# Long convolution and mixture of experts on one core: folded forward transform, y copied whole and combined a step later, loads in a ring

## Chip, cores and metric

One core of a Trainium2 chip. The metric is the device time of one execution in microseconds (us), of one launch.

## The reference, cut to what matters

```python
# B, S, D = 4, 11456, 128     E, F = 8, 1024     N = B * S
h_filt = (np.maximum(pos_emb @ w1, 0.0) @ w2) * np.exp(-0.01 * pos)[:, None]
u = x * v
y = irfft(rfft(u, n=2 * S) * rfft(h_filt, n=2 * S))[:, :S]     # along the sequence, per channel
t = (x * y).reshape(N, D)                                      # what the experts get
logits = t @ w_gate + modality_bias[modality_id]
e_idx = np.argmax(logits, axis=1)
gate_w = softmax(logits)[np.arange(N), e_idx]
out[e_idx == e] = gate_w * (np.maximum(t @ w1[e], 0.0) @ w2[e])
```

All inputs are fp32; `x` and `v` are 4 sequences of 11456 positions and 128 channels.

## The kernel before

The transform of a sequence is split into 90 x 64 points (`N1`, `N2`) and done by matmuls against constant tables. Its state is one tile `A` in SBUF (`[128, 90, 2, 128]`). The program goes through stages: the filter and its spectrum; the forward transform of sequence 0 alone (table `FIRST`); a **middle** stage (spectral product, 64-point transforms both ways); an **outer** stage, in which the inverse transform and the routing of sequence b-1 run beside the forward transform of sequence b (table `OUTER`); middle and outer in turn until sequence 3 is alone (table `LAST`); then the experts.

An outer stage has 16 steps q (`NQ`) of 8 channels. For each q:

- `load_x` (L653) and `load` (L444) bring x, u and v of q to SBUF on SP's queue, each a tile `seq` [128, 1024] from a pool of 11 buffers of 4 KB per partition (`NA`) that y and others share.
- `product` (L449), on DVE: u times v, in place. The two ways of a sequence lie in the two halves of the partitions, its two blocks `blk` in the two halves of the columns.
- `forward` (L461): for both halves h of q, four channels, two blocks and two ways: fp32 matmuls `s` of 128 rows by 64 columns, 90 moving columns (64 PE records in a step). ACT copies them to `A` (L464), one copy for each half.
- `turn0`, `turn1` (L659): 16 PE transposes `wt` out of `A` for the inverse transform, 4 copies on ACT (L660).
- `inverse` (L668): `py`, two accumulators [128, 512] in PSUM. ACT copies the second to SBUF (L671), DVE adds and subtracts it with the first, which it reads from PSUM (L673, L674), and multiplies by x into `xo` (L675): 90 points come from two halves of 45.
- routing: `half` (L716) transposes the q's half of `xo` (`xT`, copied by ACT, L718); every second step `logits` (`pl`, L724; ACT copy `lT`, L727), `lturn` (`lt`, L733), `biased` (L739), `choice` (DVE from `mx` L747 to L768, with an exponential `ex` on ACT, L751), and `send` (matmuls `pr`, `pn`, L784 to L789, positions on DVE, L791 to L798).
- POOL scatters rows of `xo` to the experts' lists by indirect DMAs (L267), each released by a DVE instruction that `paced` names.

The order is written by hand. A table names each part with its offset:

```python
OUTER = ("turn0:1 turn1:1 lturn:3 biased:3 forward:2 load_x:0 product:1 half:2 choice:3 "
         "inverse:1 logits:2 send:4 load:0 store:4 places:5")
```

`steps` (L142) issues in step t, in the table's order, part f of q = t - offset. All of PE, ACT, DVE, POOL and SP keep that order, each in its own queue. `early` and `overlapped` with `EA`, `OV`, `F1` to `F3` let a stage begin some steps before the one ahead has ended.

Of the kernel before, what the change touches and what calls it, by code (L numbers as in the profile page):

```python
# [12 lines left out]
F32 = mybir.dt.float32  # L13
# [27 lines left out]
NQ = N2 // 4  # L41
# [28 lines left out]
NA, NXO = 11, 3  # L70
# [109 lines left out]
def hyena_moe_kernel(ctx: ExitStack, tc: tile.TileContext, a: dict, out: bass.AP,  # L180
# [177 lines left out]
    with ExitStack() as cv:  # L358
# [8 lines left out]
        def new_a(name, dt=F32):  # L367
            return st.tile([D, 1024], dt, tag="a", name=name, bufs=NA)


        rings = keepp.tile([D, 12 * GW], F32, name="rings")
        A = keepp.tile([D, N1, 2, D], F32, name="A")
# [65 lines left out]
        def forward_stages(b):  # L438
            kept = {}

            def load(q):
                for name in ("u", "v"):
                    t = kept[q, name] = new_a("seq")
                    sp.dma_start(t, a[name][b, q])  # L444

            def product(q):

                u = kept[q, "u"]
                s = dve.tensor_mul(u, u, kept.pop((q, "v")))  # L449
                paced(s, 2)  # L450

            def transform(q):

                u = kept.pop((q, "u")).rearrange("p (b d n) -> p b d n", b=2, n=N2)
# [14 lines left out]
        def filter_stages():  # L469
# [3 lines left out]
            def load(q):  # L473
                t = kept[q, "emb"] = new_a("emb")[:, 0:512]
                sp.dma_start(t, a["pos_emb"][q])

            def hidden(q):
# [5 lines left out]
                r = new_a("r")[:, 0:512].rearrange("p (m f) -> p m f", m=8)  # L483
# [84 lines left out]
        def middle_stages(b):  # L568
# [16 lines left out]
            def spectrum(g):  # L585
# [3 lines left out]
                for q in range(n):  # L589
                    for c in range(2):  # L590
# [10 lines left out]
                part = [new_a("part")[:, 0:n * 4 * D].rearrange("p (c q b d) -> p c q b d", c=2, b=2, d=D)  # L601
                        for _ in range(2)]
                more = new_a("more")[:, 0:n * 4 * D].rearrange("p (i c q d) -> p i c q d", i=2, c=2, d=D)
# [43 lines left out]
        def inverse_stages(b):  # L647
# [3 lines left out]
            def load(q):  # L651
                t = kept[q] = new_a("seq")
                sp.dma_start(t, a["x"][b, q])  # L653
# [8 lines left out]
            def transform(q):  # L662
# [15 lines left out]
            return load, turn, transform  # L678
# [24 lines left out]
        def route_stages(b):  # L703
# [17 lines left out]
            def logits(o):  # L721
# [4 lines left out]
                lT = kept[o] = new_a("lT")[:, 0:4 * PU]  # L726
# [90 lines left out]
        def outer_steps(b):  # L817
# [3 lines left out]
            if b > 0:  # L821
                load_x, turn, itransform = inverse_stages(b - 1)
                rturn, logits, lturn, biased, choice, send, store, places = route_stages(b - 1)
                todo = {
                    "load_x": load_x, **by_block("turn", turn), "inverse": itransform,
# [43 lines left out]
        def place(name, shape, dt=F32):  # L869

            n = math.prod(shape)
            if not scratch or scratch[-1][1] + n > 512:
                scratch.append([new_a("scratch")[:, 0:512], 0])
# [257 lines left out]
def device_inputs(inputs):  # L1131
    arrays = {name: np.ascontiguousarray(inputs[name]) for name in _INS}
    tile4 = lambda a: a.reshape(D, 2, NQ, 4, -1).transpose(2, 0, 1, 3, 4).reshape(NQ, D, -1)
    chan8 = lambda a: a.reshape(2, 64, 2, N2, NQ, 8).transpose(4, 2, 1, 0, 5, 3).reshape(NQ, D, -1)
    for name, of, order in (("x", "x", tile4), ("u", "x", chan8), ("v", "v", chan8)):
        arrays[name] = np.ascontiguousarray(
            np.stack([order(spread(np.asarray(a))) for a in inputs[of]]))
# [27 lines left out]
```

## Time and profile before

| | us |
|---|---|
| median of 3 runs | 2307.93 (2306.96 to 2316.54) |
| the profiled execution | 2316.88 |
| its span, first to last instruction | 2315.1 |

Busy share of the span: PE 95%, PE's weight loads 76%, DVE 73%, ACT 53%, POOL 44%. The mean granted TensorE clock is 0.981. These are means over stages with different limits; the table of stages tells more. Stages in us from the start of the span: filter 0 to 103, forward transform of sequence 0 to 149, middle to 265, outer to 400, middle to 527, outer to 667, middle to 795, outer to 938, middle to 1063, sequence 3 alone to 1211, experts to the end. A step of an outer stage is read from two neighbouring `s` in PE's timeline.

### The profile page before, as it was taken

To read this page: it belongs to the slowest core of one execution; us is meant where nothing else is said; L and a number is where in the kernel's file an instruction comes from. 1 tells how busy PE (TensorE), PEld (TensorE's weight loads), DVE (VectorE), ACT (ScalarE), POOL (GpSimd) and SP (SyncE) were. 2 spreads that over 40 slices of the span, in tenths; PEclk is the share of its full clock that TensorE was granted. 3 is DMA by queue.
4 is the path that set the end of the run, shared out by engine and by line. 5 is a ranking of instruction groups with operands and counts; after the bars stand their busy time and mean duration, and the time that the engine had idled before them with its cause. 6 is when DMAs were issued, how large, how long until landed. Compare 5 with 4: busy or idle time off the path is not lost. (4 is left out here: it accounts for less than half of the span.)

```text
span 2315.1 us, 49859 instructions
## 1 busy us (share of the span) xinstructions
PE 2193.5 (95%) x18746; PEld 1758.8 (76%) x18746; DVE 1688.5 (73%) x2862; ACT 1224.2 (53%) x2245; POOL 1015.4 (44%) x1012
## 2 busy tenths in 40 slices
PE   8989999899989999898879999999999999999998
PEld 8877776677657766675447788888888888888898
DVE  2359666995679666894657677777777877777797
ACT  4632465126532365223435666666666666666676
POOL 0116300595438754396533455555553333333333
PEclk9999999999999999998879999999999999999999
DMA  9666675777867787674546622222222111111111
GB/s 309 244 253 211 220 228 177 249 252 267 272 217 256 253 267 254 213 254 143 166 133 200 219 69 76 70 67 69 67 65 73 47 47 47 47 45 46 40 42 34
DMA packets 168635, 359.22 MB, mean 155 GB/s; under 512 B 32237, under 2 KB 65497, under 8 KB 168389
## 3 DMA queue, kind: packets, MB, share of 16 engines
q1 hardware_dynamic: 141445, 295.83, 40.0%
q0 software_dynamic: 26784, 60.12, 7.4%
q8 instruction: 150, 2.46, 0.4%
q14 instruction: 96, 0.79, 0.1%
q10 hardware_dynamic: 160, 0.03, 0.0%
HBM read 271.44 MB, written 84.83 MB: 154 GB/s over the span
## 5 line engine op out<-in xcount | busy, mean ns | idle before, releaser
L1048 DVE SCALAR_TENSOR_TENSOR hl<-ph,hh 128x512 fp32r<-128x512 f32 x724 | 497.0, 690 | 217.0 <-ACT hh L1047 149.0
L1084 POOL DMA_INDIRECT out<-ot,idx x362 | 360.4, 996 | 603.6 <-DVE ot L1081 518.0
L1047 ACT ACTIVATE hh<-ph 128x512 fp32r<-128x512 f32 x724 | 433.0, 601 | 336.4 <-PE ph L1044 254.9
L267 POOL DMA_INDIRECT xs<-back,to x360 | 386.9, 1075 | 273.1 <-DVE y L673 126.1
L1042 PE MATMUL ph<-xh,wh 128*128 128x512 f32 (+1 forms) x792 | 303.4, 383 | 2.1 <-ACT wh L1013 1.2
L1065 PE MATMUL po<-hh,wh 128*128 128x512 f32 (+1 forms) x792 | 295.1, 373 | 5.4 <-ACT hh L1047 4.5
L641 ACT COPY A<-pw 128x512 f32<-128x512 f32 (+1 forms) x184 | 97.2, 580 | 379.6 <-PE pw L637 375.9
L1067 PE MATMUL po<-hl,wh 128*128 128x512 f32 (+1 forms) x792 | 295.4, 373 | 1.4 <-DVE hl L1048 1.4
L1043 PE MATMUL ph<-xh,wl 128*128 128x512 f32 (+1 forms) x792 | 295.3, 373 | 0.3 <-DVE wl L1014 0.3
L1044 PE MATMUL ph<-xl,wh 128*128 128x512 f32 (+1 forms) x792 | 295.5, 373 | 0.1
L1066 PE MATMUL po<-hh,wl 128*128 128x512 f32 (+1 forms) x792 | 294.7, 372 | 0.0
L613 DVE TENSOR_TENSOR part<-pz,rings 128x1024 f32<-128x1024 f32 (+1 forms) x184 | 211.5, 1190 | 5.3 <-POOL part L618 5.3
L593 PE MATMUL pz<-A,rings 128*64 128x256 f32 x1440 | 180.3, 393 | 31.5 <-issue 13.8
L637 PE MATMUL pw<-rings,part 64*128 64x128 f32 x2880 | 203.5, 280 | 5.7 <-POOL part L618 5.6
L637 PEld LDWEIGHTS pw<-rings,part 64*128 64x128 f32 x2880 | 177.8, 189 | 40.3 <-issue 29.5
L608 POOL TENSOR_TENSOR more<-more 128x256 f32<-128x256 f32 (+1 forms) x84 | 68.3, 813 | 284.0 <-DVE more L605 274.9
L461 PE MATMUL s<-fwd,seq 128*64 128x90 f32 x4096 | 174.2, 243 | 12.4 <-issue 4.4
L461 PEld LDWEIGHTS s<-fwd,seq 128*64 128x64 f32 x4096 | 163.1, 137 | 23.5 <-issue 6.5
L659 PEld LDWEIGHTS wt<-ident,A 128*90 128x90 f32 x1024 | 125.2, 185 | 66.3 <-issue 37.9
L1065 PEld LDWEIGHTS po<-hh,wh 128*128 128x128 f32 x792 | 149.6, 189 | 33.1 <-ACT hh L1047 5.6
L1067 PEld LDWEIGHTS po<-hl,wh 128*128 128x128 f32 x792 | 149.5, 189 | 30.0 <-DVE hl L1048 3.8
L1044 PEld LDWEIGHTS ph<-xl,wh 128*128 128x128 f32 x792 | 149.8, 189 | 26.7 <-DVE xl L1029 0.5
(172 smaller groups left out, 3788.5 us busy)
## 6 DMA issues: line engine op xcount, KB each, us to landing
rings<-hs SPq DMA_DIRECT2D x88, 512.0 KB
seq<-in_u SPq DMA_DIRECT2D x64, 512.0 KB
seq<-in_v SPq DMA_DIRECT2D x64, 512.0 KB
seq<-in_x SPq DMA_DIRECT2D x64, 512.0 KB
back<-xr SPq DMA_DIRECT2D x72, 325.0 KB
xr<-xo SPq DMA_DIRECT2D x62, 365.6 KB
rings<-in_c_b SPq DMA_DIRECT2D x88, 256.0 KB
rings<-in_c_c SPq DMA_DIRECT2D x88, 256.0 KB
```

The lines of the kernel that those rows point to most:

```text
L267: s = pool.indirect_dma_start(out=xs, out_offset=bass.IndirectOffsetOnAxis(ap=ix, axis=0), in_=src, in_offset=None, bounds_check=E * R - 1 ...
L461: pe.matmul(v[64 * c:64 * c + 64, blk, j], u[:, blk, 4 * h + j], fwd[:, c], start=True, stop=True)
L637: pe.matmul(pw[par][:, to:to + D], t[at], k["c"][at, q, c], start=i == 0, stop=i == len(terms) - 1)
L1042: pe.matmul(p, k[0, "h"][:, f:f + D], k["xh"], start=True, stop=False)
L1043: pe.matmul(p, k[0, "l"][:, f:f + D], k["xh"], start=False, stop=False)
L1044: pe.matmul(p, k[0, "h"][:, f:f + D], k["xl"], start=False, stop=True)
L1047: act.activation(hh, ph, AF.Relu)
L1048: dve.scalar_tensor_tensor(hl, ph, 0.0, hh.bitcast(F32), op0=ALU.max, op1=ALU.subtract)
L1065: pe.matmul(po, k[1, "h"][:, f], hh[:, t], start=g == 0, stop=False)
L1066: pe.matmul(po, k[1, "l"][:, f], hh[:, t], start=False, stop=False)
L1067: pe.matmul(po, k[1, "h"][:, f], hl[:, t], start=False, stop=g == NCH - 1)
L1084: s = pool.indirect_dma_start(out=out, out_offset=bass.IndirectOffsetOnAxis(ap=k["idx"][:, j:j + 1], axis=0), in_=ot[:, j, :], in_offset=N ...
```

## The change

1. **Forward on quarters, from sequence 1 on.** The product goes to a tile `p`; then `of` = [p0+p1 | p0-p1] over the two column halves: the add on DVE, the subtraction on POOL (sequence 1, and even q later) or on DVE (odd q of sequences 2 and 3). Each matmul of `forward` has 45 rows, beginning at partition 0 or 64, by 64 columns: a quarter of the array, in the order (0,0), (1,1), (1,0), (0,1) of `parts`. The number of matmuls stays. Sequence 0 keeps the old form (`whole`). For sequences 1 to 3 the host lays out u and v with the blocks in the partition halves and the ways in the column halves.
2. **y in one copy, combined a step later.** ACT copies both accumulators of `py` in one instruction of 128x1024. The new part `combine` has offset 2 in `OUTER` (first in rank) and 3 in `LAST`; it adds, forms the difference as -2 y1 + sum, and multiplies by x. `half` keeps its offset, so it now stands in the same step as the `combine` whose `xo` it reads.
3. **Loads in a ring.** x, u and v go round 7 slots of a tile `around` (sequence 0: 9 slots for u and v), two more hold `of`; the middle stages use the same slots. The first load of sequence 0 is issued from step 13 instead of 0 (`FIRST`), and outer stages begin 2 instead of 3 steps early (`EA`).

```diff
-OUTER = ("turn0:1 turn1:1 lturn:3 biased:3 forward:2 load_x:0 product:1 half:2 choice:3 "
+OUTER = ("combine:2 turn0:1 turn1:1 lturn:3 biased:3 forward:2 load_x:0 product:1 half:2 choice:3 "
          "inverse:1 logits:2 send:4 load:0 store:4 places:5")
-LAST = ("inverse:2 turn0:1 half:3 lturn:4 biased:4 logits:3 turn1:1 choice:4 load_x:1 send:5 store:5 places:6")
+LAST = ("combine:3 inverse:2 turn0:1 half:3 lturn:4 biased:4 logits:3 turn1:1 choice:4 load_x:1 send:5 "
+        "store:5 places:6")
-FIRST = "forward:17 load:0 product:16"
+FIRST = "forward:17 product:16 load:13"
-GD, OV, EA, EM = 2, 2, 3, 4
+GD, OV, EA, EM = 2, 2, 2, 4
-NA, NXO = 11, 3
+NA, NU, NS, NXO = 9, 7, 2, 3
...
         def new_a(name, dt=F32):
-            return st.tile([D, 1024], dt, tag="a", name=name, bufs=NA)
+            return st.tile([D, 1024], dt, tag="a", name=name, bufs=NS)
...
+        def rows_of(src, n=NU):
+            at = counts["rows", n] = (counts.get(("rows", n), -1) + 1) % n
+            t = around[:, at]
+            sp.dma_start(t, src)
+            return t
...
             def load(q):
                 for name in ("u", "v"):
-                    t = kept[q, name] = new_a("seq")
-                    sp.dma_start(t, a[name][b, q])
+                    kept[q, name] = rows_of(a[name][b, q], NU if b else NA)
             def product(q):
-                u = kept[q, "u"]
-                s = dve.tensor_mul(u, u, kept.pop((q, "v")))
-                paced(s, 2)
+                if b == 0:
+                    of = kept[q, "of"] = kept.pop((q, "u"))
+                    paced(dve.tensor_mul(of, of, kept.pop((q, "v"))), 2)
+                    return
+                u, v = kept.pop((q, "u"))[0:PU], kept.pop((q, "v"))[0:PU]
+                p, of = new_a("p")[0:PU], around[:, NU + q % (NA - NU)]
+                paced(dve.tensor_mul(p, u, v), 2)
+                dve.tensor_add(of[0:PU, 0:512], p[:, 0:512], p[:, 512:1024])
+                eng = pool if b == 1 or q % 2 == 0 else dve
+                eng.tensor_sub(of[0:PU, 512:1024], p[:, 0:512], p[:, 512:1024])
+                kept[q, "of"] = of
             def transform(q):
...
+                whole = [(c, blk, slice(0, D), blk) for blk in range(2) for c in range(2)]
+                parts = [(c, blk, slice(64 * blk, 64 * blk + HALF), c)
+                         for c, blk in ((0, 0), (1, 1), (1, 0), (0, 1))]
...
-                        for blk in range(2):
-                            for c in range(2):
-                                pe.matmul(v[64 * c:64 * c + 64, blk, j], u[:, blk, 4 * h + j],
-                                          fwd[:, c], start=True, stop=True)
+                        for c, blk, at, of_c in parts if b else whole:
+                            pe.matmul(v[64 * c:64 * c + 64, blk, j], of[at, of_c, 4 * h + j],
+                                      fwd[at, c], start=True, stop=True)
...
-                y = new_a("y")
-                act.copy(y[:, 512:1024], py[:, 1])
+                y = kept[q, "y"] = new_a("y")
+                act.copy(y, py.rearrange("p c m -> p (c m)"))
+            def combine(q):
+                y = kept.pop((q, "y"))
                 n = 2 if b == nb - 1 else 1
-                paced(dve.tensor_add(y[:, 0:512], py[:, 0], y[:, 512:1024]), 2 * n - 1)
-                dve.tensor_sub(y[:, 512:1024], py[:, 0], y[:, 512:1024])
-                paced(dve.tensor_mul(xo_of(b, q // 2)[:, :, q % 2, :, 0:D], four(y),
-                                     four(kept.pop(q))), n)
+                paced(dve.tensor_add(y[:, 0:512], y[:, 0:512], y[:, 512:1024]), 2 * n - 1)
+                dve.scalar_tensor_tensor(y[:, 512:1024], y[:, 512:1024], -2.0, y[:, 0:512],
+                                         op0=ALU.mult, op1=ALU.add)
+                paced(dve.tensor_mul(xo_of(b, q // 2)[0:PU, :, q % 2, :, 0:D], four(y[0:PU]),
+                                     four(kept.pop(q)[0:PU])), n)
...
```

What this does to the order of two steps in the third outer stage. On **DVE before**, from the last combination of a step with a choice through the step with the positions (`ro`, L791, and on) of a group:

```order
L673 TENSOR_TENSOR y<-py,y 128x512
L674 TENSOR_TENSOR y<-py,y 128x512
L675 TENSOR_TENSOR xo_84<-y,seq 128x2x4x128
L449 TENSOR_TENSOR seq<-seq 128x1024
L673 TENSOR_TENSOR y<-py,y 128x512
L674 TENSOR_TENSOR y<-py,y 128x512
L675 TENSOR_TENSOR xo_85<-y,seq 128x2x4x128
L791 TENSOR_TENSOR ro<-pr,base 109x128
```

On **DVE now**, the same step (`p` is the product, `around<-p` the folded sum; L821 to L828 are the positions):

```order
L702 TENSOR_TENSOR y<-y 128x512
L703 SCALAR_TENSOR_TENSOR y<-y 128x512
L705 TENSOR_TENSOR xo_84<-y,around 109x2x4x128
L467 TENSOR_TENSOR p<-around 109x1024
L468 TENSOR_TENSOR around<-p 109x512
L821 TENSOR_TENSOR ro<-pr,base 109x128
L822 TENSOR_TENSOR base<-base,pn 128x8
L823 TENSOR_TENSOR ro<-ro,oh_94 109x128
L825 TENSOR_REDUCE sl<-ro 109x16
L828 TENSOR_TENSOR ix_87<-sl,small 109x4x4
L702 TENSOR_TENSOR y<-y 128x512
```

Before, the step began with the product, and its own combination (the second) and the positions followed; now it begins with the combination of the `py` of the step ahead, and the positions stand ahead of the next combination.

On **PE now**, the end of that step (L746 is `half`, which reads the `xo` that L705 writes; the others as named above):

```order
L484 MATMUL s_9514<-fwd,around 64x90 x16
L746 MATMUL xT<-ident,xo_83 128x109 x8
L693 MATMUL py<-rings,inv 64x512 x4
L754 MATMUL pl<-rings,wg 32x436 x4
L814 LDWEIGHTS both
L814 MATMUL pr<-oh_94,both 128x128
```

PE's order is that of before; but its `xT` now reads what DVE writes in the same step.

## Rows read from the trace of the kernel before

**Rows 1.** The span cut at the stages of the program: us from the start, length, busy time and number of instructions of each engine, granted TensorE clock (1.00 is full speed), DMA share and GB/s. From above: the forward transform of sequence 0, the first and the second outer stage, and the inverse transform and routing of sequence 3 alone.

```profile
103.00:149.00 46.00, 41.07 (x1024) 40.22 (x1024) 18.61 (x18) 23.83 (x32) 0.66 (x2) 1.00 0.86 329
...
265.00:400.00 135.00, 132.41 (x1631) 95.26 (x1632) 87.56 (x177) 86.45 (x158) 0.00 (x0) 1.00 0.66 213
...
527.00:667.00 140.00, 133.78 (x1630) 95.35 (x1629) 86.73 (x177) 84.44 (x155) 67.34 (x62) 1.00 0.77 255
...
1063.00:1211.00 148.00, 119.71 (x608) 67.40 (x608) 73.61 (x174) 64.17 (x124) 72.44 (x70) 0.84 0.49 139
```

**Rows 2.** The timeline of PE through two steps of the first outer stage: start, us, engine and line, operation, out<-in, tile and shapes, count. A step starts with `s`.

```profile
321.97 2.70 PE L461 MATMUL s<-fwd,seq 128*64 128x90 f32 x64
324.60 0.97 PE L716 MATMUL xT<-ident,xo 109*128 109x109 f32 x8
325.50 1.94 PE L668 MATMUL py<-rings,inv 90*64 90x512 f32 x8
327.37 2.01 PE L659 MATMUL wt<-ident,A 128*90 128x128 f32 x16
329.31 2.70 PE L461 MATMUL s<-fwd,seq 128*64 128x90 f32 x64
...
334.70 0.94 PE L724 MATMUL pl<-rings,wg 128*32 128x436 f32 x8
335.57 0.23 PE L784 MATMUL pr<-oh,both 109*128 109x128 bf16 x1
...
335.73 2.75 PE L659 MATMUL wt<-ident,A 128*90 128x128 f32 x16
338.57 0.69 PE L733 MATMUL lt<-ident,lT 128*109 128x128 f32 x4
339.19 1.00 PE L461 MATMUL s<-fwd,seq 128*64 128x90 f32 x20
```

**Rows 3.** The same view at the start of the second outer stage, before its routing has begun: the `s` rows of two neighbouring steps.

```profile
532.98 2.70 PE L461 MATMUL s<-fwd,seq 128*64 128x90 f32 x64
...
540.31 2.70 PE L461 MATMUL s<-fwd,seq 128*64 128x90 f32 x64
```

**Rows 4.** The same view in the third outer stage: one `wt` and the same place two steps later, and between them the `xT` of the step with a `pr`, and the `pn` at the end of that group.

```profile
840.58 2.00 PE L659 MATMUL wt<-ident,A 128*90 128x128 f32 x16
...
845.52 0.97 PE L716 MATMUL xT<-ident,xo 109*128 109x109 f32 x8
...
849.28 0.18 PE L789 MATMUL pn<-sc,both 109*128 109x8 bf16 x1
...
858.61 0.59 PE L659 MATMUL wt<-ident,A 128*90 128x128 f32 x3
```

**Rows 5.** The timeline of DVE over the two steps of Rows 2 (in brackets the idle time before an instruction, and what ended it): combination, product, the choice from `mx` to the gate's column, and the positions from `ro` on.

```profile
322.09 0.28 DVE L739 TENSOR_TENSOR lg<-lt,bs 109x128 f32<-109x128 f32 x1
322.29 1.22 DVE L449 TENSOR_TENSOR seq<-seq 128x1024 f32<-128x1024 f32 x1
323.43 0.36 DVE L747 TENSOR_REDUCE mx<-lg 109x16 f32<-109x128 f32 x1
...
326.57 0.37 DVE L763 TENSOR_REDUCE se<-ex 109x16 f32<-109x128 f32 x1 [0.72 <-ACT ex L751]
...
327.35 0.12 DVE L768 TENSOR_SCALAR xo<-small 109x16 f32<-109x16 f32 x1
328.11 0.69 DVE L673 TENSOR_TENSOR y<-py,y 128x512 f32<-128x512 f32 x1 [0.65 <-ACT y L671]
328.84 0.69 DVE L674 TENSOR_TENSOR y<-py,y 128x512 f32<-128x512 f32 x1
329.56 1.23 DVE L675 TENSOR_TENSOR xo<-y,seq 128x1024 f32<-128x1024 f32 x1
330.71 1.22 DVE L449 TENSOR_TENSOR seq<-seq 128x1024 f32<-128x1024 f32 x1
...
338.03 0.28 DVE L791 TENSOR_TENSOR ro<-pr,base 109x128 f32<-109x128 f32 x1
...
339.32 0.28 DVE L739 TENSOR_TENSOR lg<-lt,bs 109x128 f32<-109x128 f32 x1
```

**Rows 6.** Groups by line and shape in the middle stage of sequence 0: operation, out<-in, count, busy us and mean ns: operations from SBUF to SBUF on 128x512, on POOL and on DVE.

```profile
L618 POOL TENSOR_TENSOR part<-part 128x512 f32<-128x512 f32 x20 | 34.4, 1719 | 16.9 <-DVE part L613 16.1 <-DMA rings<-in_c_b 0.8
...
L617 DVE TENSOR_TENSOR part<-part 128x512 f32<-128x512 f32 x22 | 15.2, 692 | 0.8
```

**Rows 7.** The same view of ACT in the first outer stage.

```profile
L464 ACT COPY A<-s 128x720 f32<-128x720 f32 x32 | 24.3, 760 | 24.1 <-PE s L461 24.1
...
L671 ACT COPY y<-py 128x512 f32<-128x512 f32 x16 | 9.5, 594 | 17.4 <-PE py L668 15.9 <-issue 1.6
```

**Rows 8.** The timeline of ACT in the third outer stage: the second copy out of `s` in a step with a choice.

```profile
858.21 0.76 ACT L464 COPY A<-s 128x720 f32<-128x720 f32 x1 [2.73 <-PE xT L716]
```

**Rows 9.** The timeline of DVE there: the sum of exponentials, which waits for ACT's `ex`.

```profile
841.77 0.39 DVE L763 TENSOR_REDUCE se<-ex 109x16 f32<-109x128 f32 x1 [2.70 <-ACT ex L751]
```

**Rows 10.** The timeline of DVE in the forward transform of sequence 0: a product.

```profile
109.28 1.23 DVE L449 TENSOR_TENSOR seq<-seq 128x1024 f32<-128x1024 f32 x1 [1.15 <-DMA seq<-in_v]
```

**Rows 11.** The timeline of DVE in the stage with sequence 3 alone.

```profile
1125.15 0.69 DVE L673 TENSOR_TENSOR y<-py,y 128x512 f32<-128x512 f32 x1 [2.56 <-ACT y L671]
```

**Rows 12.** The page's list of DMA issues: out<-in, queue, operation, count, KB each.

```profile
seq<-in_u SPq DMA_DIRECT2D x64, 512.0 KB
```

More of the change, by code (lines that the diff above doesn't have):

```diff
@@ L473, in load @@
             def load(q):
-                t = kept[q, "emb"] = new_a("emb")[:, 0:512]
+                t = kept[q, "emb"] = next_a()[:, 0:512]
                 sp.dma_start(t, a["pos_emb"][q])
@@ L482, in hidden @@
                               start=True, stop=True)
-                r = new_a("r")[:, 0:512].rearrange("p (m f) -> p m f", m=8)
+                r = next_a()[:, 0:512].rearrange("p (m f) -> p m f", m=8)
                 dve.scalar_tensor_tensor(
@@ L598, in spectrum @@
                 h = k["h"]
-                part = [new_a("part")[:, 0:n * 4 * D].rearrange("p (c q b d) -> p c q b d", c=2, b=2, d=D)
-                        for _ in range(2)]
-                more = new_a("more")[:, 0:n * 4 * D].rearrange("p (i c q d) -> p i c q d", i=2, c=2, d=D)
+                at = 3 * ((g + 1) % 3)
+                part = [around[:, at + i, 0:n * 4 * D].rearrange("p (c q b d) -> p c q b d", c=2, b=2, d=D)
+                        for i in range(2)]
+                more = around[:, at + 2, 0:n * 4 * D].rearrange("p (i c q d) -> p i c q d", i=2, c=2, d=D)
                 for i in range(2):
@@ L651, in load @@
             def load(q):
-                t = kept[q] = new_a("seq")
-                sp.dma_start(t, a["x"][b, q])
+                if q == 0:
+                    counts.pop(("rows", NU), None)
+                kept[q] = rows_of(a["x"][b, q])
             def turn(q, blk):
@@ L669, in transform @@
                                   start=True, stop=True)
-                y = new_a("y")
-                act.copy(y[:, 512:1024], py[:, 1])
+                y = kept[q, "y"] = new_a("y")
+                act.copy(y, py.rearrange("p c m -> p (c m)"))
+            def combine(q):
+                y = kept.pop((q, "y"))
                 n = 2 if b == nb - 1 else 1
-                paced(dve.tensor_add(y[:, 0:512], py[:, 0], y[:, 512:1024]), 2 * n - 1)
-                dve.tensor_sub(y[:, 512:1024], py[:, 0], y[:, 512:1024])
-                paced(dve.tensor_mul(xo_of(b, q // 2)[:, :, q % 2, :, 0:D], four(y),
-                                     four(kept.pop(q))), n)
-            return load, turn, transform
+                paced(dve.tensor_add(y[:, 0:512], y[:, 0:512], y[:, 512:1024]), 2 * n - 1)
[3 more added lines that the diff above has]
+                                     four(kept.pop(q)[0:PU])), n)
+            return load, turn, transform, combine
         md = []
@@ L725, in logits @@
                               xT_t[:, g].rearrange("p h n -> p (h n)"), start=True, stop=True)
-                lT = kept[o] = new_a("lT")[:, 0:4 * PU]
+                lT = kept[o] = st.tile([D, 4 * PU], F32, tag="lT", name="lT", bufs=1)
                 act.copy(lT, pl[:, 0:4 * PU])
@@ L871, in place @@
             n = math.prod(shape)
-            if not scratch or scratch[-1][1] + n > 512:
-                scratch.append([new_a("scratch")[:, 0:512], 0])
+            if not scratch:
+                scratch.append([rings[:, 4096:6144], 0])
             of, lo = scratch[-1]
@@ L1133, in device_inputs @@
     tile4 = lambda a: a.reshape(D, 2, NQ, 4, -1).transpose(2, 0, 1, 3, 4).reshape(NQ, D, -1)
-    chan8 = lambda a: a.reshape(2, 64, 2, N2, NQ, 8).transpose(4, 2, 1, 0, 5, 3).reshape(NQ, D, -1)
+    swap = lambda a: np.stack([a[0], a[1, :, ::-1]])
+    chan8 = lambda a: swap(a.reshape(2, 64, 2, N2, NQ, 8)).transpose(4, 0, 1, 2, 5, 3).reshape(NQ, D, -1)
+    ways8 = lambda a: a.reshape(2, 64, 2, N2, NQ, 8).transpose(4, 2, 1, 0, 5, 3).reshape(NQ, D, -1)
     for name, of, order in (("x", "x", tile4), ("u", "x", chan8), ("v", "v", chan8)):
-        arrays[name] = np.ascontiguousarray(
-            np.stack([order(spread(np.asarray(a))) for a in inputs[of]]))
+        arrays[name] = np.ascontiguousarray(np.stack([
+            (ways8 if name != "x" and b == 0 else order)(spread(np.asarray(a)))
+            for b, a in enumerate(inputs[of])]))
     pos = spread(np.asarray(inputs["pos_emb"])).reshape(2, 64, 2, NQ, 4, -1)
```

10 lines of the change are left out of this document (7 added, 3 removed).

## Prediction

> **What bounds the kernel now.** The mean shares say PE, but stages differ, so I read the span cut by stage first [rows 1]. In an outer stage PE is busy 132.41 of 135.00 and 133.78 of 140.00 us at full clock, DVE 87.56 and 86.73: PE bounds. In the stage of sequence 3 alone PE is busy 119.71 of 148.00 at a clock of 0.84, and no engine is full: a chain bounds. Experts, filter and middle stages are not touched but for buffers.
>
> Second, PE's timeline of two steps [rows 2]: `s` to `xT` takes 324.60 - 321.97 = 2.63 us, `xT` 0.90, `py` 1.87, `wt` 1.94, so 7.34 a step; every second step adds `pl` 0.87, `pr` and `pn` 0.16, `lt` 0.62. That is 16.33 of work in the 17.22 that two steps take (321.97 to 339.19); the rest is a stall inside `wt`. Before the routing begins a step takes 540.31 - 532.98 = 7.33 [rows 3]: PE alone. In the third outer stage two steps take 858.61 - 840.58 = 18.03 [rows 4]; I use that for the second stage as well, which lasts 5 us longer than the first [rows 1], as 13 such steps longer by 0.4 would.
>
> Third, DVE's timeline [rows 5], because the change loads DVE. Combination: 0.73 + 0.72 + 1.15 to the next start, 2.60. Product 1.14. Choice, `mx` to the gate's column: 327.35 + 0.12 - 323.43 - 0.72 of waiting = 3.32. Positions 339.32 - 338.03 = 1.29. `lg` 0.20. DVE's `y` waits for ACT in the first of these steps (0.65), so today it follows PE; nothing on PE waits for DVE for long, because `xT` reads an `xo` of the step before.
>
> **The forward transform.** The 64 records of a step stay, with the same 90 moving columns; only the array's part differs. Today two column halves run side by side, in 2.63 us. With four quarters at once I halve that: 1.3 less, of which I take 1.24, a first start and the gaps being kept. Bounds: nothing saved, or 1.3. The nearest row for four at once is `pl`: four column tiles, 8 records of 436 columns, mean 541 ns by itself, all done in 0.94 us [rows 2]; so four parts do overlap, even in fp32, where a matmul is two records. I take the upper value since that row is the same thing in columns.
>
> The Trainium skill ("TensorE: Matmul & The Clock Gate", Part 3, What overlaps and what doesn't) says that matmuls start and end strictly in program order. Here the two passes of an fp32 matmul come one behind the other for one quarter, so by it the second would hold back the next quarter, and the saving would be near nothing; `pl`, issued in the same manner, speaks against such a loss.
>
> Fold: the add costs DVE some 0.66 a step beyond the product (SBUF to SBUF on 128x512 took 692 ns on DVE [rows 6]), and as `of` needs all of `p`, the product itself counts 1.26 instead of 1.14. The subtraction costs the same 0.66 where it is on DVE, in one step of two in sequences 2 and 3. On POOL it takes 1.72 [rows 6]; POOL is busy 0.00 and 67.34 us in the two stages [rows 1] and has a whole step until `s` reads it: hidden. Without that cover, each microsecond would be PE's.
>
> **y.** ACT's copy grows from 128x512 (594 ns) to 128x1024. By 760 ns at 720 columns [rows 7] the slope is 0.166 / 208 columns, so 1.00 us, 0.41 more a step; ACT, busy 86.45 of 135.00, hides it. The three DVE instructions stay, now from SBUF: 2.60 as before (bounds 2.5 to 2.8).
>
> **What is late next.** Now `half` waits for `combine` in its own step, and a loop through DVE and PE appears, which I cost over two steps. Step with positions: combination 2.60, then PE's `xT`, `py`, `pl`, `pr`, 849.28 + 0.18 - 845.52 = 3.94 [rows 4], behind which `ro` waits, with only product and fold beside it; then positions 1.29: 7.83. Step with the choice: combination 2.60, `lg` 0.20, product and add 1.26 + 0.66, choice 3.32: 8.04, or 8.70 with the subtraction. With 0.1 for the hand-overs between engines: **16.0** for two steps beside sequence 1, **16.6** (I take 16.7) later. PE's own work is 16.33 - 2.48 = 13.85, so PE is no longer the bound and waits some 2.5 us in two steps. `y` of the choice step is copied by ACT behind `ex`: ready about 0.7 us before its combination, so not on the path.
>
> **The sum.** First outer stage: (17.22 - 16.0) / 2 = 0.61 a step, over some 13 steps with routing, 8. Second and third: (18.03 - 16.7) / 2 = 0.66, over 13 each, 17.3. Steps before routing stay on PE (DVE 2.60 + 1.26 + 1.32 = 5.2 is less than 6.1): 1.24 in two steps of three stages, 7.4. Together 32.7. Against it: sequence 0, where loads begin later and a product today waits 1.15 for its load [rows 10]; the stage has 46.00 - 41.07 of slack on PE: 0 to 3, I take 1. The last stage, where DVE waits 2.56 for ACT's `y` [rows 11]: the longer copy in the chain of 16 steps, 16 x 0.41 = 6.6 at most, nothing at least since `combine` comes a step later; 3, the middle. Loads: each of three a step is 512 KB [rows 12], at the stage's 255 GB/s [rows 1] 2.1 us alone and 6.2 for the three; a load of u now waits in its slot for `combine` and must be there one step later, some 8 us; a hit now and then of 1.15, 4 in all (0 to 12). Net 32.7 - 8 = 24.7. The profiled execution took 2316.88, 0.4% over the median of 2307.93; the sum leaves 2292 of the one, and of the median **2283 us**.
>
> **The rivals.**
>
> (B) The stalls stay and eat it. ACT's second copy out of `s` came 2.73 us late in a choice step [rows 8], and DVE's sum of exponentials then waited 2.70 [rows 9]; I don't know the cause. Today DVE has room for that. If a part of it (1 us in two steps) is not hidden, 26 steps give back 13; with loads at their bound nothing more than 0 to 11 is gained: 2297 to 2308, mid 2302. For it: such waits are in every choice step I read. Against it: by my sum ACT has 0.7 to spare.
>
> (C) The quarters don't run together. Then the loop through DVE is still shorter than today's 18.03, but PE's work stays 16.33 and its `s` delays `xT`: some 17.3 for two steps, 0.35 x 26 = 9, nothing in the first outer stage and before routing, minus 8: 2300 to 2310. `pl` speaks against it; that rows as well as columns are split, which no row shows, for it.
>
> (D) Slower: the late copy of `s` lands in the new loop whole. In a choice step ACT's queue is copy of `s`, `xT` copies, `ex`, `y`; all of these now stand ahead of DVE's choice and of the next combination, and `xT` behind that. If DVE waits 3 us for `ex` on top of 16.7, two steps take 19.7, 0.83 a step more than now: 26 x 0.83 = 21.6, less 8 and 7.4, plus 8 of costs: +14, 2322. A wait x makes the whole slower from 26 (x - 1.33) / 2 = 7.4 on, x = 1.9, a delay of 2.6 with the 0.7 to spare. The rows show 2.7, so this is near; but the delay is counted from the end of `s`, which now comes 1.24 earlier, and 3 us would need 3.7.
>
> (U) More: DVE's waits overlap better than in my loop, and PE's 13.85 or DVE's own sum of some 14.5 bounds: 0.8 a step more over 39 steps, 31, and half the costs gone: about 2248.
>
> **Chances.** Forecast 0.53 (its own range 2265 to 2296), B 0.17, C 0.10, D 0.12, U 0.08. About 0.5% (11.5 us) is what a measurement of this kernel tells from no change. Faster by more: all of the forecast, U, and a fifth of B: 0.64. Within: the rest of B and nearly all of C, 0.23. Slower: D and the tail of C, 0.13. The range goes from the middle of U to the near side of D: 2248 to 2318.
>
> **What would show it.** In the profile after: the `s` of a step from sequence 1 on in 1.3 to 1.5 us (C: 2.6); two steps from `wt` to `wt` in 16.0 to 16.8 us; PE idle before `xT`, released by DVE's multiplication into `xo`, some 2 us in two steps; DVE busy 98 to 105 us in an outer stage; DVE's `ro` waiting on PE's `pr` some 2 us in a group. B and D show as waits of DVE's `se` for ACT's `ex`, of 1 and of 3 us in each choice step. Products waiting for DMAs beyond 1 us in most steps would make my loads wrong, and a last stage longer than 155 us the term of that stage. I would be wrong altogether if `s` is short and two steps still take 18.

## The result

The changed kernel took 2327.66 us (median of 6 runs, 2322.65 to 2333.13), the kernel before 2309.88 beside it: ratio 1.0076, 95% interval 1.0052 to 1.0100. It is **slower** by 17.8 us, where I forecast 24.7 us less (2283) and gave "slower" 0.13; the range ended at 2318. The profiled execution has a span of 2329.3 us, 14.2 over that of before, at a mean granted clock of 0.966 (before 0.981).

The span of the changed kernel cut by stage (the columns of [rows 1]; the three outer stages and the stage of sequence 3 alone):

```profile
268.50:410.40 141.90, 121.26 (x1630) 78.27 (x1630) 106.04 (x194) 90.70 (x158) 26.68 (x16) 0.89 0.63 210
...
536.00:680.10 144.10, 123.44 (x1630) 78.21 (x1630) 106.97 (x202) 91.04 (x158) 90.71 (x71) 0.92 0.80 260
...
805.00:949.60 144.60, 126.08 (x1630) 79.62 (x1630) 106.50 (x202) 90.88 (x158) 90.70 (x71) 0.91 0.80 260
...
1074.60:1222.70 148.10, 109.18 (x606) 63.95 (x606) 75.75 (x183) 70.54 (x126) 74.78 (x72) 0.91 0.51 148
```

PE is no longer full, as I said it would be; but the clock of the outer stages, 1.00 in the first two before, is now 0.89 to 0.92. That is where part of the gain went. PE's timeline of two steps of the first outer stage (answers to [rows 2]):

```profile
316.17 1.69 PE L746 MATMUL xT<-ident,xo 109*128 109x109 f32 x8 [2.33 <-DVE xo L705]
317.79 3.68 PE L693 MATMUL py<-rings,inv 90*64 90x512 f32 x8
321.40 1.44 PE L754 MATMUL pl<-rings,wg 128*32 128x436 f32 x8
...
322.89 0.18 PE L819 MATMUL pn<-sc,both 109*128 109x8 bf16 x1
322.92 2.09 PE L684 MATMUL wt<-ident,A 128*90 128x128 f32 x16
...
325.38 1.47 PE L484 MATMUL s<-fwd,around 45*64 45x90 f32 x64
327.29 0.94 PE L746 MATMUL xT<-ident,xo 109*128 109x109 f32 x8 [0.44 <-DVE xo L705]
...
331.96 1.47 PE L484 MATMUL s<-fwd,around 45*64 45x90 f32 x64
335.75 1.36 PE L746 MATMUL xT<-ident,xo 109*128 109x109 f32 x8 [2.32 <-DVE xo L705]
337.05 3.68 PE L693 MATMUL py<-rings,inv 90*64 90x512 f32 x8
```

`s` fell from 2.70 to 1.47, so four quarters do run together. `xT` waits 2.33 and 2.32 for DVE's `xo`. Behind that wait `py` takes 3.68 in place of 1.94 [rows 2], and `pl` 1.44 in place of 0.94. The same stretch by the clock (window, length, busy time of PE, PEld, DVE, ACT and POOL, clock, DMA share, GB/s): the wait, then `xT`, `py` with the first of `pl`, `pl`, and what follows.

```profile
333.40:335.70 2.30, 0.03 (x4) 0.00 (x0) 2.23 (x4) 1.62 (x3) 0.00 (x0) 1.00 0.03 7
335.70:337.00 1.30, 1.25 (x8) 1.05 (x8) 1.20 (x2) 0.52 (x1) 0.11 (x1) 0.66 0.24 79
337.00:341.00 4.00, 4.00 (x13) 0.97 (x16) 0.54 (x1) 0.70 (x2) 1.66 (x1) 0.50 0.97 318
341.00:343.00 2.00, 2.00 (x14) 0.72 (x7) 0.29 (x1) 1.37 (x2) 0.00 (x0) 0.51 0.96 255
343.00:347.00 4.00, 3.58 (x84) 3.30 (x83) 3.76 (x9) 3.11 (x6) 0.00 (x0) 1.00 0.32 114
```

After 2.3 us of waiting the granted clock goes to 0.50, that is 1.2 in place of 2.4 GHz, for some 7 us, just while PE does the part of the loop that DVE waits for. DVE's side of it, the timeline there (answers to [rows 5]):

```profile
323.09 0.29 DVE L821 TENSOR_TENSOR ro<-pr,base 109x128 f32<-109x128 f32 x1 [5.14 <-PE pn L819]
...
324.46 0.69 DVE L702 TENSOR_TENSOR y<-y 128x512 f32<-128x512 f32 x1
...
332.94 0.68 DVE L702 TENSOR_TENSOR y<-y 128x512 f32<-128x512 f32 x1
333.65 0.69 DVE L703 SCALAR_TENSOR_TENSOR y<-y 128x512 f32<-128x512 f32 x1
334.38 1.23 DVE L705 TENSOR_TENSOR xo<-y,around 109x1024 f32<-109x1024 f32 x1
```

From `xT` at 316.17 to `xT` at 335.75 two steps take 19.58 us. Where the clock stays up (299.58 to 316.17) they take 16.59; I had 16.0. DVE's L779 (the choice takes its maximum off `lg`) is 0.68 of that: it took 0.97 us in each group of this stage, with POOL's subtraction running beside it, and 0.29 in the kernel before (L749, first line). In the second and third stages two steps at full clock took 17.67 (`xT` from 569.53 to 587.20 and from 876.69 to 894.36), where I had 16.7; there `ro` (L823) took 1.49 and 1.54 in place of 0.28 (L793), again beside POOL's subtraction. The kernel before, then the changed one:

```profile
323.82 0.29 DVE L749 TENSOR_TENSOR lg<-lg,mx 109x128 f32<-109x128 f32 x1
852.09 0.28 DVE L793 TENSOR_TENSOR ro<-ro,oh 109x128 f32<-109x128 f32 x1
```

```profile
309.33 1.41 POOL L470 TENSOR_TENSOR around<-p 109x512 f32<-109x512 f32 x1 [6.85 <-DVE p L467]
309.93 0.97 DVE L779 TENSOR_TENSOR lg<-lg,mx 109x128 f32<-109x128 f32 x1
...
881.09 1.49 DVE L823 TENSOR_TENSOR ro<-ro,oh 109x128 f32<-109x128 f32 x1
881.10 1.33 POOL L470 TENSOR_TENSOR around<-p 109x512 f32<-109x512 f32 x1
```

The sum over the three outer stages, by groups of PE's instructions (line, shapes, count, busy us, mean ns, idle time before them). Kernel before, 265 to 940 us:

```profile
L461 PE MATMUL s<-fwd,seq 128*64 128x90 f32 x3072 | 133.2, 244 | 6.5 <-ACT rings L660 3.1 <-ACT A L464 2.1 <-DVE y L674 1.1
L659 PE MATMUL wt<-ident,A 128*90 128x128 f32 x768 | 110.2, 288 | 9.6 <-issue 5.1 <-ACT A L641 2.6
L668 PE MATMUL py<-rings,inv 90*64 90x512 f32 x384 | 94.0, 605 | 0.0
L716 PE MATMUL xT<-ident,xo 109*128 109x109 f32 x384 | 46.6, 264 | 1.8 <-DVE xo L675 1.6 <-issue 0.2
L724 PE MATMUL pl<-rings,wg 128*32 128x436 f32 x188 | 24.1, 541 | 0.0
```

Changed kernel, 269 to 950 us:

```profile
L693 PE MATMUL py<-rings,inv 90*64 90x512 f32 x384 | 115.2, 722 | 0.0
L684 PE MATMUL wt<-ident,A 128*90 128x128 f32 x768 | 101.7, 284 | 3.5 <-ACT A L665 2.3 <-ACT rings L685 0.8
L484 PE MATMUL s<-fwd,around 45*64 45x90 f32 x3072 | 78.2, 242 | 4.7 <-issue 2.4 <-ACT y L696 1.8
L746 PE MATMUL xT<-ident,xo 109*128 109x109 f32 x379 | 49.6, 278 | 52.1 <-DVE xo L705 51.9
L754 PE MATMUL pl<-rings,wg 128*32 128x436 f32 x184 | 33.5, 786 | 0.0
```

`s` gives 55.0 us and its idle time 1.8, `wt` with its stall and idle time 14.6; the wait of `xT` takes 50.3 back, and `py` 21.2, `pl` 9.4 and `xT` 3.0 are the lower clock. In these five groups that adds up to 12 us more. Without the 33.6 us of the lower clock it would be some 21 less (an estimate from these sums), not the 32.7 of my sum; filler, which holds the clock up at a price of its own (below), gave back 14 to 17 in the outer stages.

The span did not grow there alone. From the first `s` of the first outer stage to the last of the third, the middle stages between them included, it is 5.6 us more (671.8 for 666.2). The other parts: 3.8 more ahead of that, 2.8 more from there to the first `wt` of the last stage, 6.6 less in that stage, and 8.6 more behind its last `wt` (1118.5 for 1109.9). What made that last part longer is not shown.

### The profile page after: what moved, and what is told of

It is laid out like the page before. It is cut to its first block, busy times and chain, and to the rows that moved or that the text cites. A ratio compares the mean times of both kernels' runs of the same rounds, so it can differ in the third digit from the quotient of the medians.

```text
span 2329.3 us, 49929 instructions
## 1 busy us (share of the span) xinstructions
PE 2155.8 (93%) x18746; PEld 1705.2 (73%) x18746; DVE 1738.2 (75%) x2926; ACT 1241.3 (53%) x2245; POOL 1084.1 (47%) x1044
## 4 chain that ended last, share of the span: by engine, by line
PE 53%; issue 24%; DVE 13%; POOL 6%; DMA 2%; ACT 1%; SPq 0%; POOLq 0%; DVEq 0%; ACTq 0%; another core or an unknown queue 0%
PE pw L661 10%; PE pz L616 7%; POOL out L1114 5%; PE py L693 4%; PE po L1097 3%; PE po L1095 3%; PE ph L1074 3%; PE ph L1073 3%; PE ph L1072 3%; PE po L1096 3%; PE s L484 2%; DVE xo L705 2%; PE pl L754 2%; PE xT L746 2%; DVE y L702 1%
## 5 line engine op out<-in xcount | busy, mean ns | idle before, releaser
L268 POOL DMA_INDIRECT xs<-back,to x360 | 409.5, 1137 | 223.8 <-DVE y L702 106.0
L661 PEld LDWEIGHTS pw<-rings,around 64*128 64x128 f32 x4320 | 248.3, 188 | 37.4 <-issue 31.1
L661 PE MATMUL pw<-rings,around 64*128 64x128 f32 x4320 | 265.6, 276 | 3.6 <-POOL around L642 3.4
L637 DVE TENSOR_TENSOR around<-pz,rings 128x1024 f32<-128x1024 f32 (+1 forms) x184 | 211.4, 1190 | 0.0
L1096 PEld LDWEIGHTS po<-hh,wl 128*128 128x128 f32 x792 | 149.5, 189 | 25.9
L1072 PEld LDWEIGHTS ph<-xh,wh 128*128 128x128 f32 x792 | 149.9, 189 | 25.2 <-ACT wh L1043 1.4
L1073 PEld LDWEIGHTS ph<-xh,wl 128*128 128x128 f32 x792 | 150.2, 190 | 23.6 <-DVE wl L1044 0.6
L616 PEld LDWEIGHTS pz<-A,rings 128*64 128x64 f32 x1440 | 102.1, 140 | 83.9 <-issue 28.2
```

The source lines that it names most:

```text
L268: s = pool.indirect_dma_start(out=xs, out_offset=bass.IndirectOffsetOnAxis(ap=ix, axis=0), in_=src, in_offset=None, bounds_check=E * R - 1 ...
L616: pe.matmul(pz[at, q, 2 * D * c:2 * D * c + 2 * D], k["b"][:, 2 * q + par, 64 * c:64 * c + 64], A[:, G * g + 2 * q + par].rearrange("p b d ...
L661: pe.matmul(pw[par][:, to:to + D], t[at], k["c"][at, q, c], start=i == 0, stop=i == len(terms) - 1)
L1072: pe.matmul(p, k[0, "h"][:, f:f + D], k["xh"], start=True, stop=False)
L1073: pe.matmul(p, k[0, "l"][:, f:f + D], k["xh"], start=False, stop=False)
L1096: pe.matmul(po, k[1, "l"][:, f], hh[:, t], start=False, stop=False)
```

## The experiments

Groups of runs fell on different chips, on which the kernel before itself took 2246 to 2310 us; so each run is set against the kernel before on its own chip, and stages are compared within a group. The table has ratio and interval, and from the traces the us from the first to the last `s` of outer stages 1, 2, 3 and from the first to the last `wt` of the stage with sequence 3 alone. A trace is of one execution; those of e5 and e6 are slower than their medians (2255.23 for 2245.35, 2262.17 for 2253.94).

| run | ratio to before | outer 1, 2, 3 | last |
|---|---|---|---|
| kernel before, changed kernel (first chip) | 1.0076 | 128.4, 134.1, 135.8; 132.1, 134.7, 135.4 | 142.1; 135.6 |
| e4_filler | 1.0155 (1.0134 to 1.0176) | 121.2, 133.2, 133.2 | 124.2 |
| e2_half_later | 1.0106 (1.0077 to 1.0134) | 108.1, 125.8, 126.6 | 124.2 |
| e3_combine_same | 1.0235 (1.0213 to 1.0257) | 123.8, 135.2, 134.1 | 125.1 |
| e1_whole | 1.0071 (1.0050 to 1.0092) | 121.2, 123.9, 123.9 | 125.6 |
| r_before | one run, 2247.93 | 128.4, 128.3, 128.3 | 98.1 |
| r_after | 1.0242 (1.0225 to 1.0259) | 134.3, 134.2, 132.6 | 124.6 |
| e5_quarters_only | 0.9987 (0.9977 to 0.9997) | 120.8, 129.5, 123.3 | 99.0 |
| e6_quarters_half_later | 1.0022 (1.0010 to 1.0034) | 112.1, 127.9, 137.2 | 98.3 |
| e9_last_only | 1.0068 (1.0049 to 1.0087) | 132.7, 135.0, 135.5 | 128.6 |
| e7_whole_last | 0.9858 (0.9823 to 0.9892) | 121.2, 125.8, 125.9 | 137.3 |
| e8_half_later_last | 0.9975 (0.9949 to 1.0002) | 108.9, 129.4, 127.8 | 126.5 |
| e10_first_quarters | 0.9879 (0.9853 to 0.9904) | 108.6, 125.9, 125.4 | 139.1 |
| r2_after | 1.0161 (1.0138 to 1.0185) | 132.1, 133.6, 135.0 | 132.1 |
| e4_again | 1.0057 (1.0035 to 1.0079) | 121.2, 131.9, 133.7 | 128.4 |
| e11_filler_all | 1.0099 (1.0071 to 1.0127) | 121.3, 131.6, 131.4 | 143.9 |
| e7_again | 0.9908 (0.9879 to 0.9937) | 121.3, 126.0, 125.6 | 123.8 |
| e12_combine_only | 0.9845 (0.9797 to 0.9893) | 121.6, 122.3, 122.6 | 123.4 |
| e13_ring_only | 0.9945 (0.9919 to 0.9972) | 127.4, 132.4, 134.3 | 126.1 |

**Filler.** If the clock makes `py` slow, useless work for PE in the wait must make the kernel faster.

```diff
                     pt = bank("xT")
+                    for h in range(16 if half == 1 and way == 0 and b < nb - 1 else 0):
+                        pe.transpose(pt[:, D * (h % 4):D * (h % 4) + D], ident, ident)
```

> The changed kernel with 16 more PE transposes of the identity (128x128, some 0.12 us each, 1.9 in all) ahead of xT in each step with a pr, into the bank that xT overwrites: work for PE in the 2.2 us in which it waits for DVE's combine; nothing else is changed. Clock theory: PE's wait before xT is what lets the clock fall to 1.2 GHz, so that py takes 3.68 and pl 1.68 in place of 1.94 and 0.94, on the loop. Then with more work for PE py is back at 1.94 in nearly all steps, two steps take 16.6 in place of 19.6 beside sequence 1, and the time falls by 25 to 45 us to 2285 to 2303. Rival, contention: py is slow because DVE, ACT and POOL read and write beside it; then py stays at 3.68 and the time is the same or up to 10 us longer. Rival, the loop alone: the time is the same within 4 us.

> The changed kernel, unchanged, on the chip of the two runs with filler: 1.006 to 1.026 of the kernel before, py slow in most groups of the three outer stages.

> 16 more transposes ahead of xT in each outer step with a pr, as before. Clock theory: two steps in the first outer stage 16.5 us as against 19.6 in the changed kernel of this group, with the stage 10 to 13 us shorter; in the second and third the wait of the other step remains and the gain is 0 to 5 each: 10 to 25 us less than the changed kernel. Contention or the loop alone: no stage shorter, the time equal or up to 30 us longer (1.97 us in 24 steps).

On one chip the changed kernel took 2324.13 us, with filler 2299.61; 14 of the 24.5 us lie in the three outer stages, where the filler is. Two steps in the first outer stage (filler on L746, `xT` now L748; run e4_filler):

```profile
320.89 0.94 PE L748 MATMUL xT<-ident,xo 109*128 109x109 f32 x8 [0.41 <-DVE xo L705]
...
326.97 1.97 PE L746 MATMUL xT<-ident 128*128 128x128 f32 x16
329.27 0.97 PE L748 MATMUL xT<-ident,xo 109*128 109x109 f32 x8 [0.33 <-DVE xo L705]
330.16 1.94 PE L693 MATMUL py<-rings,inv 90*64 90x512 f32 x8
332.03 0.94 PE L756 MATMUL pl<-rings,wg 128*32 128x436 f32 x8
...
337.42 0.94 PE L748 MATMUL xT<-ident,xo 109*128 109x109 f32 x8 [0.44 <-DVE xo L705]
```

With 1.97 us more to do, PE takes 16.53 for two steps in place of 19.58, at `py` 1.94, beside the same DVE, ACT and POOL: it is the wait that slows `py`, through the clock, and not what runs beside it. In the second and third stages the wait of the other step stays, hence 1 to 2 us there. (Beside the first run of it there was no changed kernel on its chip; its forecast in us was made for the first chip.)

> As the run ahead of it, and 10 more transposes (1.2 us) ahead of xT in the other steps from the second outer stage on, and 20 and 10 in the last stage: 59 us of useless work on PE in all over the kernel with the change. Clock theory: the clock stays near full in all outer stages and the last, py at 1.94 and pl at 0.94 in nearly all groups; 25 to 60 us less than the changed kernel. Contention: it is longer than the run with 16 alone by most of the added work, 15 to 35 us.

Filler in both steps (`range(0 if way else (20 if b == nb - 1 else 16) if half else 10 if b else 0)`) holds `py` and `pl` at their old means throughout; PE's groups over the outer stages, first with 16, then with all:

```profile
L693 PE MATMUL py<-rings,inv 90*64 90x512 f32 x384 | 99.6, 635 | 0.0
...
L756 PE MATMUL pl<-rings,wg 128*32 128x436 f32 x192 | 24.7, 541 | 0.0
```

```profile
L693 PE MATMUL py<-rings,inv 90*64 90x512 f32 x384 | 93.9, 605 | 0.0
...
L756 PE MATMUL pl<-rings,wg 128*32 128x436 f32 x192 | 24.7, 541 | 0.0
```

The gain over the changed kernel is 13.7, not the 25 to 60 that I expected: the last stage, with filler as well, grew to 143.9 from 132.1, and in the outer stages the second filler gives 0.3 and 2.3 in the second and third. Even with `py` at its old mean these two stages take 131.6 and 131.4, so the clock is not all that keeps them long.

**One part alone.** The changed kernel without quarters and fold (`if True` for `if b == 0` in the product, `whole` for `parts`, the host's old layout):

> The changed kernel without quarters and fold: product in place, s in the old form for all sequences, everything else as changed. Clock theory: PE keeps 16.33 us of work in two steps, the loop through DVE has 15.1 (no fold), so PE waits little, the clock stays full, py 1.94; two steps 16.5 to 17.3, time 2300 to 2318. If the combination a step later or the ring by itself is what costs, it is 2320 or more and xT still waits 1 us or more in each group.

Outer stages at 121 to 124, `py` at 605 ns: without quarters nothing falls. It is still 1.0071, with the last stage at 125.6 (below). The kernel before with quarters and fold alone (p in place in u, `of` over v):

> The kernel before with quarters and fold alone (product in place in u, folded halves written over v): y, its place and the pool of loads as before. If the combination a step later is what opens the wait of xT, this one keeps xT on the xo of the step before: two steps 14.8 to 16, 25 to 45 us faster than the kernel before. If a shorter s alone makes PE wait for the combination (behind py: ACT's copy 0.6 and 2.6 of DVE, beside wt 1.94 and s 1.44) and lets the clock fall, py is slow in most groups, and it is between 10 us faster and 25 us slower.

Nearly nothing, -0.13%: neither of my cases wholly (the time lies in the range of the second, `py` is slow in some groups only). The first outer stage is 7.6 shorter than before on that chip, the second 1.2 longer: with a shorter `s` alone PE waits at other places, in the second stage 8.3 us ahead of `s` for DVE's y, and `py` is at 634 and 666 ns in these two stages.

**The step in which `half` stands.** In the changed kernel the combination back behind its `inverse` (`inverse:1 combine:1`), and `half`, `logits`, `choice` and what follows one step later (`half:3`, `logits:3`, `choice:4`, `send:5` ...), the latter on the kernel before with quarters too:

> The changed kernel with combine in the step of its inverse and behind it in rank (offset 1), as before the change, but with quarters, one copy of y and the ring. Loop theory: xT reads the xo of the step before again; behind py stand ACT's copy 1.0 and the combination 2.6, beside PE's wt 1.94 and s 1.44, so PE waits 0.3 to 0.6 a step; two steps 14.8 to 16.0, clock near full, 2268 to 2295. If the shorter s alone is enough to let the clock fall, py stays slow in most groups and it is 2310 to 2330.

> The changed kernel with half, lturn, biased, logits, choice, send, store and places one step later, so that xT reads an xo that combine wrote a step before. Clock and loop theory: PE no longer waits for DVE in its own step; the wait of xT goes (0.5 or less), py stays at 1.94, two steps are bound by DVE's 14 to 14.5 us or PE's 13.85 and take 14.5 to 15.8; over 39 steps 0.9 to 1.3 a step against before: 2265 to 2290. Rival, contention: py still 3.68 in some steps, two steps 17 or more, 2305 to 2330. Rival, loads: products wait for DMAs for more than 1 us a step as soon as steps are shorter, 2290 to 2310.

> The run with quarters alone, and half, lturn, biased, logits, choice, send, store and places one step later. Theory: xT waits for nothing, two steps are bound by DVE's 14 to 14.5 us: 15 to 16, and the time is 15 to 45 us below the kernel before, with py at 1.94 where PE doesn't wait. Rival: PE, with 13.85 of work under a DVE that needs 14.5, waits at another place (s for of) and the clock falls there as well: within 10 us of the kernel before.

With `half` later the first outer stage takes 108 to 112, as the loop's end should give; but later stages, where DVE has its subtractions and POOL its scatters, stay at 126 to 137, and in e2 the hand-over through a middle stage is 6 us longer (last `s` to the next first `s` 139.3 and 138.0 in place of 133.0 and 132.1 in e1). In e2's second stage `s` waits 6.0 us for POOL's subtraction:

```profile
L484 PE MATMUL s<-fwd,around 45*64 45x90 f32 x832 | 21.3, 241 | 6.2 <-POOL around L470 6.0 <-DVE around L470 0.2
```

The combination put back with quarters (e3) helps little: the first outer stage is shorter, 123.8, but the whole stands at 1.0235 (1.0242 for the changed kernel on another chip); `xT` still waits 13.3 and 13.4 us in the first two stages, and `pl` is at 698 and 710 ns.

**The last stage.** For each kernel on its chip:

> The kernel before, unchanged, for its trace on the chip of this group. Stage by stage it should be at PE's 16.33 us of work for two steps, 16.4 to 18. In the group of runs ahead of this, on another chip, the kernel before took 2246 us; if its stages there were shorter in all parts, the outer stages here take some 121 to 124 us from the first to the last s in place of 128 to 136, and the last stage some 10 us less. On a chip like the first it is within 0.4% of 2308.

> The changed kernel, unchanged, beside the others of this group. Clock theory: py at 3.7 us in most groups of all three outer stages, PE's granted clock 0.88 to 0.93 there, and 0.5 to 2.5% slower than the kernel before; the more, the closer the kernel before comes to PE's floor on this chip (up to 2.5% where its outer stages take 121 to 124 us). Rival: the loss is in loads or in the first stage, then it is 0.5 to 1% whatever the chip.

> The changed kernel with the last stage alone put back: combine directly behind its inverse (LAST with combine:2), the outer stages as changed. Loop and clock theory: in the stage of sequence 3 alone xT waits for the same step's combination as well, up to 3.4 us, the clock falls and py and pl take up to twice as long; put back, the stage takes 98 to 102 us from the first to the last wt in place of 125, and the run is 22 to 32 us faster than the changed kernel: 1.010 to 1.015 of the kernel before on the chip of the second group (where the change stood at 1.024). If ACT's longer copy of y is what costs there, 118 us or more remain.

On that chip the last stage takes 98.1 in the kernel before and 124.6 in the changed one, 98 to 99 in e5 and e6, which leave this stage as it was. Windows in the kernel before, and in the changed one, with an `xT` there:

```profile
1070.00:1095.00 25.00, 25.00 (x162) 16.10 (x161) 21.94 (x55) 16.30 (x33) 19.68 (x18) 1.00 0.72 222
1095.00:1120.00 25.00, 23.38 (x142) 14.01 (x141) 17.69 (x48) 14.42 (x30) 19.52 (x19) 1.00 0.69 205
```

```profile
1100.00:1130.00 30.00, 23.65 (x142) 14.76 (x142) 15.86 (x40) 14.63 (x27) 18.19 (x18) 0.89 0.62 184
1130.00:1160.00 30.00, 22.81 (x124) 13.48 (x123) 16.36 (x43) 14.07 (x26) 17.67 (x18) 0.83 0.58 166
```

```profile
1136.88 1.69 PE L746 MATMUL xT<-ident,xo 109*128 109x109 f32 x8 [3.37 <-DVE xo L705]
```

The same wait, 3.37 us here, and the same fall of the clock. But on the first chip the kernel before already ran this stage at 0.84 [rows 1], and there the changed one is 6.5 shorter; and with the old table (`LAST` with `inverse:2 combine:2`) on another chip it took 128.6 as well. The forecast for e9 missed, and its rival stands: e9 keeps ACT's longer copy of y, and no run has the old table with that copy on the chip of r_before. So what cost 26 us there, the step of the combination or the copy, is not separated; the trace speaks for the first (`xT` waits 22.9 us for DVE's `xo` in that stage, in r_before not at all).

The chips themselves differ in one thing at least that the traces show. In the kernel before on the first chip PE stood still in this stage 12.5 us, in five places, while it waited for nothing that the profile shows ("issue"); in r_before it did not. The stage of e9 has such pauses too (`wt` 3.1, `lt` 2.4). What they are stays open. (In the line: us in total, times, longest.)

```profile
PE pl L724 <- issue: 12.5, 5, 5.0
```

**What of the change pays.** With the old table in `LAST`:

> The run without quarters and fold, with the last stage put back as well: what is left of the change is the copy of y, the combination a step later in the outer stages, and the ring. Theory: PE at its 16.33 in the outer stages (121 to 124 us from the first to the last s), the last stage back at 98 to 102: 2263 less 25 to 32, 0.989 to 0.995 of the kernel before. If the last stage is slow for another reason it stays at 1.005 or more.

> The run with quarters and half one step later in the outer stages, with the last stage put back: 2270 less 22 to 32, 0.990 to 1.001 of the kernel before. Set beside the run without quarters and with the last stage put back it says what quarters are worth once nothing waits in its own step: by the sum of the prediction 1.24 x 48 = 60 us less, by DVE's work of 14.5 in two steps 20 less in the first outer stage and nothing later, where the clock falls.

> Quarters and half one step later in the first outer stage alone (there POOL makes all subtractions), the other stages without quarters, the last stage put back. Theory: the first outer stage 108 us from the first to the last s in place of 121, its hand-over to the middle stage some 6 longer, so 5 to 9 us less than without quarters: 0.985 to 0.992 of the kernel before. If a shorter outer stage only moves the wait to the middle stage, it is within 3 us of the run without quarters.

> Without quarters and fold, last stage put back: 0.980 to 0.992 of the kernel before, py at 1.94 in the outer stages, and 30 to 75 us below the changed kernel of this group.

Without quarters the kernel beats both, by 1.4 and 0.9% of the kernel before on two chips, and by 57 us the changed kernel on the second (2266.95 against 2324.13). Quarters everywhere, with `half` later (e8), lose most of that; in the first stage alone they save 13 there and give 7.5 back in the hand-over, no gain in the whole that can be told. Which of the remaining parts pays:

> The kernel before with y in one copy and the combination a step later in the outer stages (in the last stage directly behind its inverse); s, the pool of loads and the loads of sequence 0 as before. If the combination a step later takes the stall of 0.9 out of wt (two steps 16.2 to 16.4 in place of 17.2), it alone brings the gain of the best version: 0.984 to 0.993 of the kernel before, with the outer stages at 121 to 126 us from the first to the last s. If the ring does, it stays at 0.997 to 1.003.

> The best version with the combination in the step of its inverse in the outer stages too: the ring and the one copy alone. If the combination a step later brings the gain: 0.997 to 1.005 of the kernel before, the stall in wt (some 0.9 in two steps) back. If the ring does: 0.984 to 0.993.

The combination a step later is the gain (0.9845); the edit is part 2 of the change put into the kernel before, with `inverse:2 combine:2` in `LAST`. Beside it on the same chip stands e13, with the ring in place of the later step and y in one copy like e12: e12 is 25.4 us faster (2271.04 and 2296.41), with 27.6 us less in the three outer stages. PE's `wt` in a step with routing, in e7_again and two steps on, is without the stall of [rows 2] (2.75):

```profile
318.45 2.09 PE L684 MATMUL wt<-ident,A 128*90 128x128 f32 x16
...
334.66 2.09 PE L684 MATMUL wt<-ident,A 128*90 128x128 f32 x16
```

Two steps take 16.21, PE's work and no more. With the combination put back (e13) `wt` is at 2.75 again; the ring and the one copy together stand 0.5% (0.3 to 0.8) below the kernel before.

## Why the prediction was wrong

- **The forward transform**: right. 1.24 a step was forecast, 55.0 / 48 = 1.15 measured; rival C fell. The Trainium skill ("TensorE: Matmul & The Clock Gate", Part 3, What overlaps and what doesn't) has matmuls in program order; the two records of an fp32 matmul did not keep the next quarter back here.
- **The loop through DVE and PE**: its path was right, down to `ro` waiting for `pr` and `xT` waiting for `combine`, and at full clock its length nearly so beside sequence 1 (16.59 for 16.0). Later it was 17.67 for 16.7, so by the prediction's own formula, (18.03 - 17.67) / 2 x 26, those two stages had 4.7 us to give at full clock, not 17.3.
- **The step that failed** is the PE part of that loop, "849.28 + 0.18 - 845.52 = 3.94". It is taken from a PE that never waits, and I used it for a PE that, by my own sum in the same paragraph, "waits some 2.5 us in two steps". In its place stand 322.89 + 0.18 - 316.17 = 6.90 us, 2.96 more, as the clock halves behind the wait. The loop so becomes 19.58, longer than the 17.22 of before there [rows 2]: a short `s` with two steps above 18 was my sign of being wrong altogether. I had the warning: the stage of [rows 1] with PE at 119.71 of 148.00 has a clock of 0.84, and I read it as a chain of that stage only. No rival had it; the sign I gave to D belongs to another mechanism.
- The Trainium skill (the same page, Part 1, What's actually happening) says that TensorE's clock is throttled unless the engine has lately been busy. The trace agrees: 1.00 before the wait, 0.50 behind it.
- **Rivals B and D**: wrong in mechanism. `se` no longer waits for `ex`, and the late copy of `s` did not land in the loop.
- **POOL**: I had its subtraction hidden. Its length was right (1.7 beside sequence 1), but a DVE instruction in the loop took 0.68 to 1.26 us longer while it ran (L779, L823 above). That is read from the traces alone; no run takes the subtraction off POOL.
- **ACT, loads**: hidden as said; no product waits for a DMA by 1 us a step. The last `s` of sequence 0 ended at 152.5 in place of 148.7 on the first chip, 147.0 in place of 146.5 on that of r_before; there it ended at 152.5 in e5 too, which leaves sequence 0 as it was, so the change is not shown to cost anything here.
- **The last stage**: +3 forecast; 6.5 less on the first chip, 26 more on another, with the same wait in its trace.

## What to carry to other kernels

A saving on the engine that bounds opens waits on it, and TensorE's waits are not free: what it does right behind them may run at half the clock. So where a sum makes PE wait inside a loop, cost PE's part of the loop at both clocks before believing the gain; if the longer one exceeds today's step, the change can lose, as it did here. What paid was the combination a step later, which takes a stall out of `wt`, with PE's work left as it was (e12). With PE's work made shorter as well, most of that was lost again in the later outer stages and the hand-overs, even where `half` too stood a step later (e8).

## What was not expected of the hardware

Waits of 2.31 to 2.34 us were followed by a granted clock of 0.50, some 7 us long, in 4 of the 7 groups of the first outer stage, and waits of 0.68 to 1.94 in the other three were not. The length of the wait does not settle it: in the second stage one of 2.24 left `py` at 1.94, in the third one of 1.77 was followed by a `py` of 2.92. With 16 useless transposes (1.97 us) in that wait the whole took 24.5 us less. And the kernel before took from 2246 to 2310 us on different chips; of the 69 us between the two traces of it, 44 are the last stage, 98.1 to 142.1.
